# Up-projections of five of six blocks by a one-level Strassen product

## The chip, the cores and the metric

The kernel runs on one core of one Trainium2 chip. The metric is the device time of one execution in microseconds (us). Times quoted are medians. TensorE is called PE, VectorE DVE, ScalarE ACT, GpSimd POOL, and SyncE, which issues the transfers, SP.

## The reference

A Mamba-2 scan over 4 batches of 8 heads and 768 steps gives 3072 tokens of 256 features. A max-out feed-forward layer follows. Only the second part changes:

```python
def _moe_ref(x, w1, w2, w3, w_out) -> np.ndarray:      # x: 3072 x 256, w1..w3: 256 x 768, w_out: 768 x 256
    h = np.maximum(np.maximum(x @ w1, x @ w2), x @ w3)
    return (h @ w_out).astype(np.float32)
```

All of it is float32.

## The kernel before

Six blocks of 512 tokens are worked off. In each block PE runs the up-projections of its tokens (`up`), the down-projection (`down`), and between them the scan steps of the next block: transposes (`trB`, `trC`), scores (`s`), the state (`A`) and the scan's output (`y`). The order of instructions on each engine is written by hand. A bank is one tile of PSUM, the memory that PE writes its results to. A record is one entry of the trace: each float32 matmul leaves two.

```python
    def att_bank(shape, name):
        return ps.tile(shape, FP32, tag="att", bufs=5, name=name)
    def ffn_bank(shape, name):
        return ps.tile(shape, FP32, tag="ffn", bufs=3, name=name)
    # ... cut ...
    def up(c, f):                       # 128 of the 768 hidden features, 512 tokens
        # ... cut ...
        for i in range(3):              # w1, w2, w3
            p = ffn_bank([P, BLK], "up")
            for k in range(KD):         # two halves of the 256 input features
                nc.tensor.matmul(
                    out=p, lhsT=w_sb[i][:, k, f * P:(f + 1) * P], rhs=yT[c][:, k],
                    start=(k == 0), stop=(k == KD - 1))
            if i == 0:
                m = ffn.tile([P, BLK], FP32, tag="m", bufs=3, name="m")
                nc.scalar.copy(out=m, in_=p)
            else:
                nc.vector.tensor_tensor(
                    out=m if i == 1 else hT[c][:, f], in0=m, in1=p, op=ALU.max)
            fill()                      # a piece of decoding or of the scan's decays, on ACT and POOL
    def down(c, u):
        o = ffn_bank([P, 2, DM], "o")
        for i in range(2):
            # ... cut ...
            for f in range(NF):
                nc.tensor.matmul(
                    out=o[:, i], lhsT=hT[c][:, f, b * P:(b + 1) * P], rhs=wo_sb[:, f],
                    start=(f == 0), stop=(f == NF - 1), skip_group_check=True)
```

In the first block the weights are also decoded, by ACT, DVE and POOL in turn, while PE already multiplies.

## Time and profile before

| | |
|---|---|
| time, median of 3 | 320.5 us |
| span of the profiled execution | 318.6 us |
| PE busy | 303.2 us, 95% |
| DVE, ACT, POOL busy | 36%, 35%, 17% |
| one block in the middle | 48.6 us, PE never waits |

In the profile a group is a source line with its engine and tiles: "out<-in" names the tiles, "x" counts instructions; "idle before" is the time in which the engine waited just ahead of them, and the releaser is what ended it.

### The profile page before, as it was taken

Reading aid. Unit: us, or ns where it says so; the run is one execution under the profiler, and the core shown is the slowest. Engines: PE = TensorE matmul, PEld = TensorE weight load, DVE = VectorE, ACT = ScalarE, POOL = GpSimd, SP = SyncE. Lnnn points to the kernel's source line nnn. Section 1 sums busy time; section 2 is a strip of 40 time slices with the busy share of each in tenths; the row PEclk is TensorE's granted clock in tenths of the full one; section 3 lists DMA queues with packets and bytes.
Section 4 is the critical chain, followed back from the end, with each engine's and each line's share of the span. In section 5 each row is a group of like instructions: output and inputs, shape, how many; then the busy total and the mean of one; then the engine's idle time right before and its main releaser. Section 6 shows DMA issues by size and latency. Waiting matters only on the chain.

```text
span 318.6 us, 4456 instructions
## 1 busy us (share of the span) xinstructions
PE 303.2 (95%) x1746; PEld 173.7 (55%) x1746; DVE 113.2 (36%) x189; ACT 112.5 (35%) x276; POOL 54.0 (17%) x58
## 2 busy tenths in 40 slices
PE   6779998969999999999999999999999999999995
PEld 4533453458444478544468544468544468544474
DVE  2697673930133440123540123540023540023110
ACT  2857369534640264240174240084331001110100
POOL 5134563570000340000250000150000000000000
PEclk9999999979999999999999999999999999999999
DMA  8996989991798001569001569001000001000001
GB/s 90 244 389 177 173 245 197 198 106 35 196 170 97 0 1 35 161 174 128 1 0 35 147 185 129 2 2 35 33 1 0 0 2 35 33 0 0 0 0 66
DMA packets 105012, 28.06 MB, mean 88 GB/s; under 512 B 75296, under 2 KB 101920, under 8 KB 104992
## 3 DMA queue, kind: packets, MB, share of 16 engines
q1 hardware_dynamic: 104688, 27.66, 41.5%
q8 instruction: 13, 0.21, 0.3%
q10 hardware_dynamic: 304, 0.13, 0.1%
q14 instruction: 7, 0.06, 0.1%
HBM read 24.54 MB, written 3.24 MB: 87 GB/s over the span
## 4 chain that ended last, share of the span: by engine, by line
PE 82%; DVE 6%; ACT 4%; DMA 2%; POOL 2%; issue 1%; SPq 1%; ACTq 0%; DVEq 0%; POOLq 0%
PE up L502 51%; PE o L519 20%; PE y L479 3%; PE s L449 3%; DVE L L458 2%; PE y L471 2%; ACT L L367 2%; PE spread L298 1%; DMA E<-cums 1%; DVE w_u L158 1%; POOL w_u L167 1%; ACT w_u L157 1%; DVE w L170 1%; ACT CT L399 1%; PE trC L388 1%
## 5 line engine op out<-in xcount | busy, mean ns | idle before, releaser
L502 PE MATMUL up<-yT,w 128*128 128x512 f32 x432 | 190.2, 595 | 1.5 <-DVE w L170 1.5
L502 PEld LDWEIGHTS up<-yT,w 128*128 128x128 f32 x432 | 80.7, 190 | 98.4 <-issue 90.2
L519 PE MATMUL o<-wo,h 128*128 128x256 f32 x288 | 67.2, 390 | 3.2 <-DVE wo L170 3.2
L519 PEld LDWEIGHTS o<-wo,h 128*128 128x128 f32 x288 | 54.9, 194 | 14.2 <-DVE wo L170 4.0
L509 DVE TENSOR_TENSOR m<-m,up 128x512 f32<-128x512 f32 x36 | 24.7, 687 | 100.0 <-PE up L502 71.7
L507 ACT COPY m<-up 128x512 f32<-128x512 f32 x36 | 21.0, 584 | 106.4 <-PE up L502 106.4
L367 ACT ACTIVATE L<-L,ncums 128x128 f32<-128x128 f32 x160 | 48.8, 390 | 12.6 <-POOL L L363 12.6
L509 DVE TENSOR_TENSOR h<-m,up 128x512 f32<-128x512 f32 x36 | 24.7, 687 | 29.1 <-PE up L502 28.8
L458 DVE TENSOR_TENSOR L<-s,L 128x512 f32<-128x512 f32 x48 | 29.7, 682 | 3.5 <-PE s L449 3.5
L523 ACT COPY ob<-o 128x512 f32<-128x512 f32 x12 | 7.0, 585 | 49.4 <-PE o L519 41.4
L167 POOL TENSOR_TENSOR w_u<-w_u,w_r 128x512 uint32<-128x512 uint32 x12 | 18.1, 1505 | 31.3 <-DVE w_u L161 30.3
L363 POOL TENSOR_SCALAR_AFFINE_SELECT L<-L 128x1024 f32<-128x1024 f32 x20 | 21.6, 1112 | 0.0
L449 PE MATMUL s<-CT,BT 32*128 32x256 f32 x192 | 14.3, 399 | 2.9 <-ACT CT L399 2.9
L449 PEld LDWEIGHTS s<-CT,BT 32*128 32x128 f32 x192 | 9.3, 184 | 11.4 <-issue 6.8
L435 POOL TENSOR_TENSOR old<-S,E 128x256 f32<-128x256 f32 x4 | 2.5, 619 | 74.5 <-issue 74.5
L479 PE MATMUL y<-L,raw_x 128*32 128x128 f32 x384 | 13.7, 275 | 1.2 <-DVE L L458 1.1
L485 DVE COPY yT<-y 128x512 f32<-128x512 f32 x5 | 3.5, 692 | 31.7 <-PE y L479 31.7
L479 PEld LDWEIGHTS y<-L,raw_x 128*32 128x32 f32 x384 | 10.5, 109 | 4.1 <-DVE L L458 3.2
L438 POOL TENSOR_TENSOR S<-S,old 128x256 f32<-128x256 f32 x4 | 3.2, 800 | 47.7 <-DVE S L430 47.7
L158 DVE TENSOR_SCALAR w_u<-w_u 128x512 f32<-128x512 f32 x12 | 6.7, 555 | 10.9 <-ACT w_u L157 10.9
L485 ACT COPY yT<-y 128x512 f32<-128x512 f32 x7 | 4.0, 586 | 11.6 <-PE y L479 11.6
L157 ACT ACTIVATE w_u<-rb 128x512 f32<-128x512 f32 x12 | 8.0, 670 | 0.1
(66 smaller groups left out, 111.9 us busy)
## 6 DMA issues: line engine op xcount, KB each, us to landing
L<-cums SPq DMA_DIRECT2D x10, 1024.0 KB, 9.1
rb<-in_moe_w_dram SPq DMA_DIRECT2D x9, 512.0 KB, 7.7
raw_x<-in_x_dram SPq DMA_DIRECT2D x6, 512.0 KB, 7.3
out_dram<-ob SPq DMA_DIRECT2D x12, 256.0 KB, 2.1
raw_B<-in_B_dram SPq DMA_DIRECT2D x6, 256.0 KB, 4.3
raw_C<-in_C_dram SPq DMA_DIRECT2D x6, 256.0 KB, 6.2
rb<-in_moe_w_out_dram SPq DMA_DIRECT2D x3, 512.0 KB, 5.7
E<-cums SPq DMA_DIRECT2D x40, 32.0 KB, 4.0
```

Of the source, the lines that this page charges most:

```text
L157: nc.scalar.activation(u.bitcast(FP32), hi.bitcast(FP32), AF.Abs)
L158: nc.vector.tensor_scalar(out=u.bitcast(FP32), in0=u.bitcast(FP32), scalar1=SMALL, scalar2=LARGE, op0=ALU.max, op1=ALU.min)
L167: nc.gpsimd.tensor_tensor(out=u, in0=u, in1=r, op=ALU.add)
L363: nc.gpsimd.affine_select(out=L[:, b], in_=L[:, b], pattern=[[0, NH], [1, P]], compare_op=ALU.is_ge, fill=MASKED, base=0, channel_multipli ...
L367: nc.scalar.activation(L[:, b, h], L[:, b, h], AF.Exp, bias=ncum[c][:, b * NH + h:b * NH + h + 1], scale=1.0)
L449: nc.tensor.matmul(out=banks[r][:, i].rearrange("j g i -> j (g i)"), lhsT=st["BT"][rows, b], rhs=st["CT"][rows, b].rearrange("p g i -> p ( ...
L458: nc.vector.tensor_tensor(out=M, in0=banks[r], in1=M, op=ALU.mult)
L479: nc.tensor.matmul(out=ys[t][q * D:(q + 1) * D, b], lhsT=st["x"][:, b * NH + h], rhs=M[:, b, h], start=(c == 0 and b == 0), stop=True, til ...
L502: nc.tensor.matmul(out=p, lhsT=w_sb[i][:, k, f * P:(f + 1) * P], rhs=yT[c][:, k], start=(k == 0), stop=(k == KD - 1))
L507: nc.scalar.copy(out=m, in_=p)
L509: nc.vector.tensor_tensor(out=m if i == 1 else hT[c][:, f], in0=m, in1=p, op=ALU.max)
L519: nc.tensor.matmul(out=o[:, i], lhsT=hT[c][:, f, b * P:(b + 1) * P], rhs=wo_sb[:, f], start=(f == 0), stop=(f == NF - 1), skip_group_check ...
```

## The change

Strassen's scheme makes a product of two 2x2 block matrices from 7 block products in place of 8, at the price of sums before and after. Here the blocks are 128x128 of weights by 128x256 of tokens. The sums of weights (`wsum`) are made once, those of tokens (`T`) once a block, and the results are combined by DVE. Three of the four banks of a unit are accumulated on further: product 6 goes onto product 1, product 4 onto product 7, product 3 onto product 5. What ACT copies of products 1 and 6 together is called s2, and DVE's sum of s2 and product 7 is u3. Between the accumulation steps the partial sums are read, so products depend on each other through ACT and DVE; the scan steps are placed between them. Five units of one or two such groups of seven products make up a block.

```diff
-    wraw = ctx.enter_context(tc.tile_pool(name="wraw", bufs=9))
+    wraw = ctx.enter_context(tc.tile_pool(name="wraw", bufs=7))
-        return ps.tile(shape, FP32, tag="att", bufs=5, name=name)
+        return ps.tile(shape, FP32, tag="att", bufs=4, name=name)
+    def own_bank(tag, shape, name):
+        return ps.tile(shape, FP32, tag=tag, bufs=2 if tag == "u" else 1, name=name)
-            r = wtmp.tile(shape, U32, tag="w_r", name="w_r")
+            r = wtmp.tile(shape, U32, tag="w_r", bufs=1, name="w_r")
# ... cut: weight sums, T, and the bookkeeping of a unit ...
+        def p6(self):
+            self.product(6, "u")                       # onto product 1
+            self.s2 = self.kept("s2")                  # ACT copies the bank
+            u3 = ffn.tile([P, 2, HBLK], FP32, tag="u3", bufs=1, name="u3")[:, 0:self.w]
+            nc.vector.tensor_tensor(
+                out=u3, in0=self.banks["e"][:, 0:self.w], in1=self.s2, op=ALU.add)
+            self.result(1, 1, "d", u3)
+        def p4(self):
+            self.product(4, "e")                       # onto the bank that u3 reads
+            self.result(1, 0, "e", self.s2)
# ... cut ...
+        for n, unit in enumerate(units):
+            follows = units[n + 1] if n + 1 < len(units) else None
+            unit.p6()
+            fill()
+            if follows:
+                follows.p1()
+            between[n][0]()                            # a scan step
+            unit.p4()
+            unit.p3()
+            behind = between[n][1:]
+            for step in behind[0:2]:                   # scan weights, on DVE
+                step()
+            if follows:
+                follows.p7()
+                follows.p5()
+                follows.p2()
+            maxima()                                   # the maxima over w1, w2, w3, put off to here
+            for step in behind[2:]:
+                step()
# ... cut: in block 1 ...
+            weight_sums(0, nc.vector)
             scan_weights(1, 2, scan_scores(1, 2))
```

Block 1 keeps the plain up-projection. Blocks 2 to 6 use the products.

More of the change, by code (lines that the diff above doesn't have):

```diff
@@ L56 @@
     BLK = NB * P
+    HBLK = BLK // 2
+    NQ = NF // 2
     QH = P // D
@@ L73, in att_bank @@
     def att_bank(shape, name):
-        return ps.tile(shape, FP32, tag="att", bufs=5, name=name)
+        return ps.tile(shape, FP32, tag="att", bufs=4, name=name)
+    def own_bank(tag, shape, name):
+        return ps.tile(shape, FP32, tag=tag, bufs=2 if tag == "u" else 1, name=name)
+    turns = []
     def ffn_bank(shape, name):
-        return ps.tile(shape, FP32, tag="ffn", bufs=3, name=name)
+        turns.append(None)
+        return own_bank(("u", "d", "u", "e")[(len(turns) - 1) % 4], shape, name)
     a_rows = a.rearrange("b h s -> (b h) s")
@@ L376 @@
     yT = {}
+    sides = {}
     def scan_b(c, bank):
@@ L453, in scan_scores, with scan_weight, scan_old @@
         return banks
+    def scan_weight(c, b0, r, bank):
+        M = Ls[c][:, b0:b0 + 2, 2 * r:2 * r + 2]
+        nc.vector.tensor_tensor(out=M, in0=bank, in1=M, op=ALU.mult)
     def scan_weights(c, b0, banks):
         for r in range(NP):
-            M = Ls[c][:, b0:b0 + 2, 2 * r:2 * r + 2]
-            nc.vector.tensor_tensor(out=M, in0=banks[r], in1=M, op=ALU.mult)
-    def scan_out(c):
+            scan_weight(c, b0, r, banks[r])
+    def scan_old(c, bs):
         st = blocks[c]
-        M = Ls[c]
-        yT[c] = ffn.tile([P, KD, BLK], FP32, tag="yT", name="yT")
-        ys = [att_bank([P, NB, P], "y") for _ in range(KD)]
+        if "y" not in st:
+            st["y"] = [att_bank([P, NB, P], "y") for _ in range(KD)]
         if c > 0:
+            ys = st["y"]
             Sp = states[c]
-            for b in range(NB):
+            for b in bs:
                 for r in range(NP):
@@ L475, in scan_out @@
                         skip_group_check=True)
+    def scan_out(c):
+        st = blocks[c]
+        M = Ls[c]
+        ys = st["y"]
+        yT[c] = ffn.tile([P, KD, BLK], FP32, tag="yT", bufs=1, name="yT")
         for b in range(NB):
@@ L485, in scan_out @@
             copy(out=yT[c][:, t], in_=ys[t].rearrange("p b i -> p (b i)"))
+        if c > 0:
+            y11, y12, y21, y22 = (
+                yT[c][:, k, r * HBLK:(r + 1) * HBLK] for k in range(2) for r in range(2))
+            late = [ys[k].rearrange("p b i -> p (b i)")[:, r * HBLK:(r + 1) * HBLK]
+                    for k in range(2) for r in range(2)]
+            t = ffn.tile([P, 4, HBLK], FP32, tag="T", bufs=1, name="T")
+            for k, (a1, a0) in enumerate((
+                    (late[1], y11), (late[3], t[:, 0]), (late[3], y12), (late[2], t[:, 1]))):
+                nc.vector.tensor_tensor(out=t[:, k], in0=a1, in1=a0, op=ALU.subtract)
+            sides[c] = {1: y11, 2: y21, 3: y22, 4: t[:, 3], 5: t[:, 0], 6: t[:, 1], 7: t[:, 2]}
     hT = {}
@@ L496, in up @@
         if f == 0:
-            hT[c] = ffn.tile([P, NF, BLK], FP32, tag="h", name="h")
+            hT[c] = ffn.tile([P, NF, BLK], FP32, tag="h", bufs=1, name="h")
         m = None
@@ L505, in up @@
             if i == 0:
-                m = ffn.tile([P, BLK], FP32, tag="m", bufs=3, name="m")
+                m = ffn.tile([P, BLK], FP32, tag="t", bufs=6, name="m")
                 nc.scalar.copy(out=m, in_=p)
@@ L511, in up, with weight_sums @@
             fill()
+    UNITS = [[(0, 0), (0, 1)], [(1, 0), (1, 1)], [(2, 0), (2, 1)], [(0, 2), (1, 2)], [(2, 2)]]
+    wsum = const.tile([P, 4, 3, NQ, P], FP32, name="wsum")
+    def weight_sums(i, eng):
+        a11, a12, a21, a22 = (
+            w_sb[i][:, k].rearrange("p (q g f) -> p g q f", g=2, f=P)[:, g]
+            for g in range(2) for k in range(2))
+        s1, s2, s3, s4 = (wsum[:, k, i] for k in range(4))
+        eng.tensor_tensor(out=s1, in0=a21, in1=a22, op=ALU.add)
+        eng.tensor_tensor(out=s3, in0=a11, in1=a21, op=ALU.subtract)
+        eng.tensor_tensor(out=s2, in0=s1, in1=a11, op=ALU.subtract)
+        eng.tensor_tensor(out=s4, in0=a12, in1=s2, op=ALU.subtract)
@@ new lines, in left, with __init__, product, kept @@
+    def left(k, i, q):
+        if k in (1, 2, 4):
+            g, row = {1: (0, 0), 2: (0, 1), 4: (1, 1)}[k]
+            f = 2 * q + g
+            return w_sb[i][:, row, f * P:(f + 1) * P]
+        return wsum[:, {5: 0, 6: 1, 7: 2, 3: 3}[k], i, q]
+    class Unit:
+        def __init__(self, c, n):
+            self.c, self.n = c, n
+            self.quads = UNITS[n]
+            self.w = len(self.quads)
+            self.banks = {}
+        def product(self, k, into, tag=None):
+            if tag is not None:
+                shape = [P, 2, HBLK]
+                self.banks[into] = (
+                    att_bank(shape, "p_" + into) if tag == "att" else own_bank(tag, shape, "p_" + into))
+            for j, (i, q) in enumerate(self.quads):
+                nc.tensor.matmul(
+                    out=self.banks[into][:, j], lhsT=left(k, i, q), rhs=sides[self.c][k],
+                    start=(tag is not None and j == 0), stop=True, skip_group_check=True)
+        def kept(self, name):
+            t = ffn.tile([P, 2, HBLK], FP32, tag="kept", bufs=3, name=name)[:, 0:self.w]
+            nc.scalar.copy(out=t, in_=self.banks["u"][:, 0:self.w])
+            return t
+        def result(self, g, r, into, other):
+            h = hT[self.c].rearrange("p (q g) (r t) -> p q g r t", g=2, r=2)
+            i, q = self.quads[0]
+            bank = self.banks[into][:, 0:self.w]
+            if i == 0 and q == 0:
+                nc.vector.tensor_tensor(out=h[:, 0:2, g, r], in0=bank, in1=other, op=ALU.add)
+                return
+            t = ffn.tile([P, 2, HBLK], FP32, tag="t", bufs=6, name="t")[:, 0:self.w]
+            nc.vector.tensor_tensor(out=t, in0=bank, in1=other, op=ALU.add)
+            if q == 0:
+                dst, a0, a1 = h[:, 0:2, g, r], h[:, 0:2, g, r], t
+            elif self.w == 2:
+                dst, a0, a1 = h[:, q, g, r], t[:, 0], t[:, 1]
+            else:
+                dst, a0, a1 = h[:, q, g, r], h[:, q, g, r], t[:, 0]
+            later.append(lambda: nc.vector.tensor_tensor(out=dst, in0=a0, in1=a1, op=ALU.max))
+        def p1(self):
+            self.product(1, "u", "u")
+            self.s1 = self.kept("s1")
+        def p2(self):
+            self.product(2, "b", "att")
+            self.result(0, 0, "b", self.s1)
+        def p5(self):
+            self.product(5, "d", "d")
+        def p7(self):
+            self.product(7, "e", "e")
+        def p6(self):
[8 more added lines that the diff above has]
+            self.result(1, 0, "e", self.s2)
+        def p3(self):
+            self.product(3, "d")
+            self.result(0, 1, "d", self.s2)
@@ new lines, with maxima, up_all @@
+    later = []
+    def maxima():
+        while later:
+            later.pop(0)()
+    def up_all(c, between):
+        hT[c] = ffn.tile([P, NF, BLK], FP32, tag="h", bufs=1, name="h")
+        units = [Unit(c, n) for n in range(len(UNITS))]
+        for p in (Unit.p1, Unit.p2, Unit.p7, Unit.p5):
+            p(units[0])
+        for n, unit in enumerate(units):
[17 more added lines that the diff above has]
+                step()
@@ L521, in down @@
                     start=(f == 0), stop=(f == NF - 1), skip_group_check=True)
-        ob = ffn.tile([P, 2, DM], FP32, tag="ob", bufs=3, name="ob")
+        ob = ffn.tile([P, 2, DM], FP32, tag="ob", bufs=2, name="ob")
         nc.scalar.copy(out=ob, in_=o)
@@ L534 @@
     spread_j((0, 1))
-    spread_banks(2, (att_bank, ffn_bank))
+    spread_banks(2, 2 * [ffn_bank])
     spread_i((2,), True)
@@ L551 @@
     s01 = scan_scores(0, 0)
-    s23 = scan_scores(0, 2, [att_bank] + 3 * [ffn_bank])
+    s23 = scan_scores(0, 2, 4 * [ffn_bank])
     scan_weights(0, 0, s01)
@@ L556 @@
     decode()
+    scan_old(0, ())
     scan_out(0)
-    for _ in range(6):
+    for _ in range(4):
         fetch()
@@ L565 @@
     decay_load(1)
+    fetch()
+    fetch()
     load(1, "B")
@@ L590 @@
                 d[2], lambda: (sign(), d[3](), d[4]()), decode, d[5], decode, d[6], decode, d[7]]
-    for c in range(NC):
-        n = c + 1
-        for k, (g, i) in enumerate(pieces):
-            if g is down:
-                sign()
-            g(c, i)
-            if c == 0 and k == 1:
-                first_tokens()
-                scan_state(0)
-            if n < NC:
-                in_, s01, s23, state, out_ = (3, 4, 5, 5, 6) if c == 0 else (1, 3, 5, 4, 6)
-                if k == in_:
-                    scan_b(n, att_bank)
-                    scan_c(n, att_bank)
-                    if n < NC - 1:
-                        scan_bd(n)
-                if k == max(in_, s01 - 2 * (c > 0)):
-                    scan_cd(n)
-                if k == s01:
-                    scan_weights(n, 0, scan_scores(n, 0))
-                if k == s23:
-                    scan_weights(n, 2, scan_scores(n, 2))
-                if k == state and n < NC - 1:
-                    scan_state(n)
-                if k == out_:
-                    scan_out(n)
-            if n + 1 < NC and k == 4:
-                decay_load(n + 1)
-                last_load(n + 1)
-                load(n + 1, "B")
-                load(n + 1, "C")
-                load(n + 1, "x")
-                fillers += decays_of(n + 1)
@@ new lines, in loads @@
+    def loads(c):
+        if c < NC:
+            load(c, "B")
+            load(c, "C")
+            last_load(c)
+            decay_load(c)
+            load(c, "x")
+            fillers.extend(decays_of(c))
+    for k, (g, i) in enumerate(pieces):
+        if g is down:
+            sign()
+        g(0, i)
+        if k == 1:
+            first_tokens()
+            scan_state(0)
+        if k == 3:
+            scan_b(1, att_bank)
+            scan_c(1, att_bank)
+            scan_bd(1)
+        if k == 4:
+            scan_cd(1)
+            scan_weights(1, 0, scan_scores(1, 0))
+            loads(2)
+        if k == 5:
+            weight_sums(0, nc.vector)
+            scan_weights(1, 2, scan_scores(1, 2))
+            scan_state(1)
+        if k == 6:
+            scan_old(1, range(NB))
+            scan_out(1)
+            weight_sums(1, nc.gpsimd)
+            weight_sums(2, nc.vector)
@@ new lines, in transposed, with scores, weighted @@
+    def transposed(c):
+        if c < NC:
+            scan_b(c, att_bank)
+            scan_c(c, att_bank)
+            scan_cd(c)
+            if c < NC - 1:
+                scan_bd(c)
+    transposed(2)
+    for c in range(1, NC):
+        n = c + 1
+        held = {}
+        def scores(k):
+            held[k] = scan_scores(n, k)
+        loads(n + 1)
+        def weighted(k):
+            return [lambda r=r: scan_weight(n, k, r, held[k][r]) for r in range(NP)]
+        steps = [(nothing,)] * len(UNITS)
+        if n < NC:
+            steps = [
+                (lambda: scores(0), *weighted(0)),
+                (lambda: scan_state(n) if n < NC - 1 else None,),
+                (lambda: transposed(n + 1),),
+                (lambda: scores(2), *weighted(2)),
+                (lambda: scan_old(n, (0, 1)), lambda: scan_old(n, (2, 3))),
+            ]
+        up_all(c, steps)
+        down(c, 0)
+        if n < NC:
+            scan_out(n)
+        down(c, 1)
```

## The prediction

> **What bounds the kernel now.** I read the page's busy shares first, then the groups of instructions, then the chain of work in order of time, and last the timeline around one block, for latencies.
>
> ```profile
> PE 303.2 (95%) x1746; PEld 173.7 (55%) x1746; DVE 113.2 (36%) x189; ACT 112.5 (35%) x276; POOL 54.0 (17%) x58
> ...
> L502 PE MATMUL up<-yT,w 128*128 128x512 f32 x432 | 190.2, 595 | 1.5 <-DVE w L170 1.5
> ...
> L519 PE MATMUL o<-wo,h 128*128 128x256 f32 x288 | 67.2, 390 | 3.2 <-DVE wo L170 3.2
> L519 PEld LDWEIGHTS o<-wo,h 128*128 128x128 f32 x288 | 54.9, 194 | 14.2 <-DVE wo L170 4.0
> L509 DVE TENSOR_TENSOR m<-m,up 128x512 f32<-128x512 f32 x36 | 24.7, 687 | 100.0 <-PE up L502 71.7
> L507 ACT COPY m<-up 128x512 f32<-128x512 f32 x36 | 21.0, 584 | 106.4 <-PE up L502 106.4
> ```
>
> PE is the bound, DVE and ACT idle two thirds of the time. A block has 6x3x2 = 36 up matmuls and the six blocks 216, so 432 records say that each float32 matmul is two records. Means overlap (pipelining), so I take pace from the chain, here block 4 of 6:
>
> ```profile
> 177.09 10.30 PE up L502 x24
> 187.39 0.44 PE trB L388 x4
> 187.83 0.44 PE trC L388 x4
> 188.27 10.30 PE up L502 x24
> 198.57 1.08 PE s L449 x16
> 199.65 5.35 PE up L502 x12
> 204.99 0.58 PE A L423 x32
> 205.58 5.35 PE up L502 x12
> 210.92 1.08 PE s L449 x16
> 212.00 5.38 PE o L519 x24
> 217.38 1.03 PE y L471 x32
> 218.41 1.89 PE y L479 x64
> 220.29 5.38 PE o L519 x24
> ```
>
> Nothing but PE, without a gap: 48.6 us a block. A 512-column record costs 10.30/24 = 0.429 us, a 256-column record 5.38/24 = 0.224, not half of 0.429. Only the first block (to 79.9 us) has PE waits.
>
> For the waits to come I need the other engines' latencies (timeline of block 3, and a group of the forms view):
>
> ```profile
> 151.15 2.48 DVE L458 TENSOR_TENSOR L<-s,L 128x512 f32<-128x512 f32 x4 [0.44 <-PE s L449]
> 156.34 0.65 PE L423 MATMUL A<-raw_x,Bd 128*32 128x64 f32 x32
> 156.45 0.69 DVE L509 TENSOR_TENSOR h<-m,up 128x512 f32<-128x512 f32 x1 [0.96 <-PE up L502]
> 159.43 5.95 ACT L367 ACTIVATE L<-L,ncums 128x128 f32<-128x128 f32 x20
> ```
>
> ```profile
> L170 DVE SCALAR_TENSOR_TENSOR wo<-rb,w_u 128x512 uint32<-128x512 uint32 x3 | 2.0, 682 | 0.0
> ```
>
> So: DVE starts 0.11 us after the next PE work starts (156.45-156.34). One 512-wide two-input DVE operation lasts 0.69, a queue of them paces at (2.48-0.69)/3 = 0.60. A two-input operation with everything in SBUF lasts as long (0.68). An ACT copy of a bank lasts 0.58; ACT exponentials pace at 0.30. PE restarts about 0.06 after what it waited for (scores at 51.85 after the CT copies end at 51.79). For 256 columns the rows give 0.42 (state update, 128x256); its pace, by the 0.60 at 512[...], I estimate at 0.33.
>
> **What the Trainium skill says.** "VectorE: DVE Perf Modes", section "The perf-mode tier table", has tensor_tensor on float32 at 1x wherever its operands lie; the 0.60 pace from PSUM and 0.68 duration in SBUF agree, so moving the maxima to SBUF makes them no faster. "TensorE: Matmul & The Clock Gate", section "Architectural detail: the array is 16x 32x32, not 1x 128x128", calls ACT and DVE strict FIFO. The trace before cannot prove it, but everything below rests on it: a DVE instruction that is ready still waits for those queued ahead. The same page, section "LDWEIGHTS (loading the stationary operand)", gives columns/1.2 ns, 107 ns for 128; this trace shows 190 to 194 for float32, so the measurement decides. A load that long behind a 0.21 us matmul is my reading of why a 256-column record takes 0.224 and not 0.215.
>
> **The change part by part.**
>
> *Products removed.* Per block 36 matmuls of 512 columns (72 x 0.429 = 30.9 us) become 9 groups x 7 products of 256 columns, 126 records x 0.224 = 28.2 us. Gain 2.7 us a block, 13.4 us over five. The shorter moving side takes a third of the 1/8 that Strassen promises. Scan work on PE keeps its amount and only moves.
>
> *Combination added.* Before, a block needed 12 DVE maxima and 6 ACT copies. Now each of five units has four result adds, one u3 add and four maxima (five fewer in the first): 41 DVE operations, about 23 us a block, plus four subtractions. Total DVE time still fits into 50 us, so the question is where the operations stand.
>
> *The dependent products.* Product 4 accumulates onto the bank that u3 reads, so PE waits for product 6 -> ACT copy s2 -> DVE u3. Counted from the end of product 6: 0.11+0.58+0.06+0.69+0.06 = 1.50 us. In between PE has the next unit's product 1 (4 records, 0.90) and a scan step (scores 1.08, state 0.58, transposes 0.88). That would nearly cover it, and is the intent. But the DVE order of the changed kernel shows, between one unit's last result and the next unit's u3: the result of the next unit's product 2, then the four deferred maxima. That result cannot start before product 2 ends, and product 2 is just ahead of product 6. So all maxima run at the worst moment while DVE idled before. From the end of product 2:
> - DVE: 0.11 + 0.60 (result) + 4x0.60 (maxima) + 0.69 (u3) + 0.06 = 3.86.
> - PE: product 6 0.90 + product 1 0.90 + transposes 0.88 = 2.68. Wait 1.18 us (third unit).
> - Second unit: one maximum, but two scan-weight multiplies: 3.26 against 2.38, wait 0.88.
> - Fourth unit: three wide and one half maximum 3.59, against 0.90+0.45+1.08 = 2.43, wait 1.16.
> - Fifth unit, half width: 0.11+0.33+4x0.33+2x0.60 (weights)+0.42+0.06 = 3.44, against product 6 0.45 and half the old-state matmuls 0.52: wait 2.47. Its short products 5 and 2 also come too early for the banks being read: 0.40 + 0.15.
> - First unit: 1.50 against 0.90+1.08: none.
>
> *A second wait.* In the third unit the DVE multiply Cd is queued before the result of product 4. Cd waits for ACT, which first does s2, four exponentials, s1, BT, two CT and E: about 4.7 us after product 6. The result then ends at about 6.0 and frees the bank for the next product 7, which PE would reach at 4.75: 1.3 us, in blocks 2 to 4.
>
> *Sums.* Blocks 3, 4: 0.88+1.18+1.16+0.55+2.47+1.3 = 7.5 of waits less 2.7, so +4.8; adding up the stages gives +4.5, as PE work shifts a little. I take 4.5. Block 2 also holds the transposes moved forward, +5.4. Block 5 lacks state and transposes to fill with, and the Cd wait: +4.1. Block 6 has no scan step at all: waits 0.6+0.6+2.06+2.24+0.40+1.79 = 7.7, less 2.7, so +5.0. Five blocks: 5.4+4.5+4.5+4.1+5.0 = +23.5.
>
> *First block.* Eight weight sums of 384 columns go to DVE (estimate from the same pace, 0.46 each, 3.7 us; half of them ahead of the scan weights and the last decoding step that its down-projection waits for) and four to POOL; two weight loads come after the first scan loads; a single w_r buffer makes ACT wait for POOL (1.5 us per addition). Other engines already hold PE there: I put +3, with little precision.
>
> 320.5 + 23.5 + 3 = 347; I name 346.
>
> **The rivals.**
> - *PE bound throughout, as intended:* the waits are hidden and only products count: 320.5 - 13.4 + a few for the first block = 309. For it: DVE is 36% busy, and the scan steps (0.58 to 1.08) are just what covers 1.50. Against: the order of the maxima, and nothing to cover in block 6.
> - *Half hidden:* maxima run faster than 0.60, at 0.33 say. Then the second to fourth units wait some 0.1 to 0.4, the fifth about 2; near 4 a block, against 2.7 gained: about 325. Against: the 0.68 of an all-SBUF operation.
> - *DVE and POOL contend, or the clock drops:* the decode's one-input operation took 1.50 us once, where its mean is 0.555, beside a POOL addition. If POOL's masks slow the maxima so, or the granted clock, 1.00 in all later blocks, suffers from gaps of 1 to 2.5 us: 355 or more.
> - *First block decides:* the memory now taken for sums delays the decode by 5 us or more. It adds to any of the others.
>
> **Range and chances.** The gain of 13 us is nearly certain; the waits, 37 us by my sums, could be off by a third, and the first block by 3. So 332 to 357. Within 2% (314 to 327) needs the waits halved; faster by over 2% needs nearly all of them hidden. Chances: faster 0.05, within 2% 0.08, slower 0.87.
>
> **What would show it.** Product records at 0.224; in a middle block a unit-to-unit period of about 3.9+4.5 = 8.3 us; PE's idle time before product 4 ended by DVE, the largest before the fifth unit, and u3's start right at the end of a maximum or weight multiply; idle before product 7 ended by the result behind Cd; block length about 53 us, the last block's up part 36 against 30.9. I am wrong if DVE idles before u3 (then ACT or the banks set it), if PE shows no idle in blocks 3 to 6, or if the products pace below 0.21.

## The result

| | before | changed |
|---|---|---|
| time, median | 319.99 us (4 runs) | 376.54 us (4 runs, 374.79 to 379.90) |
| span, profiled execution | 318.6 us | 373.1 us |
| mean granted clock of TensorE | 0.995 | 0.929 |

The ratio is 1.178 (95% interval 1.168 to 1.189): the mean time of one kernel's fast runs over that of the other's of the same rounds, so not quite the ratio of the medians. Executions over 1.5% slower than the fastest of the same kernel are left out of the means. The change costs 56.5 us, where 25.5 were predicted and 357 was the upper end of the range.

These lines of the changed kernel's page answer to those of before: busy shares; the row of the granted clock, one digit for each fortieth of the span; and the group of product 4.

```profile
PE 313.8 (84%) x2016; PEld 232.5 (62%) x2016; DVE 203.7 (55%) x362; ACT 120.9 (32%) x296; POOL 60.5 (16%) x62
...
PEclk9989985889998989998989999989999989998899
...
L581 PE MATMUL p_e<-T,w 128*128 128x256 f32 x90 | 27.7, 427 | 36.5 <-DVE u L628 36.5
```

PE is busy 10.6 us longer than before, though it multiplies less, and idle 59 us where it was idle 15. A single releaser holds 36.5 us of that: the DVE addition u3 ahead of product 4 (`p_e<-T,w`). And the clock row has 8s in every block.

The third unit of block 3 shows both. First PE in the timeline (start, duration, engine, line, operation, tiles, size, count; in brackets the idle time before it and what ended it):

```profile
168.62 0.60 PE L397 MATMUL trB<-ident,raw_B 128*128 128x128 f32 x4
169.05 0.60 PE L397 MATMUL trC<-ident,raw_C 128*128 128x128 f32 x4
172.70 1.33 PE L581 MATMUL p_e<-T,w 128*128 128x256 f32 x4 [3.04 <-DVE u L628]
173.82 1.91 PE L581 MATMUL p_d<-yT,wsum 128*128 128x256 f32 x4
175.52 1.72 PE L581 MATMUL p_e<-T,wsum 128*128 128x256 f32 x4
```

Then DVE in the same stretch:

```profile
167.16 0.69 DVE L601 TENSOR_TENSOR t<-p_b,s 128x512 f32<-128x512 f32 x1 [2.16 <-PE p_b L581]
167.77 4.27 DVE L608 TENSOR_TENSOR h<-h,t 128x512 f32<-128x512 f32 x4
171.96 0.68 DVE L628 TENSOR_TENSOR u<-p_e,s 128x512 f32<-128x512 f32 x1
```

DVE sits idle for 2.16 us until product 2 (`p_b`) is done. Then it does that result, the four maxima, and only then u3, for which s2 had been copied by ACT at about 168.5. This is the queue order that the prediction named. New are two sizes: the maxima take 4.27 us instead of the 2.4 assumed, and after the wait of 3.04 us four product records take 1.91 us where others take 1.03.

The windows view sets the clock beside this: a middle block of the kernel before, and of the changed kernel block 1, block 3, and the 4.5 us behind that wait (the columns are busy time of each engine, then PEclk, DMA share, GB/s).

```profile
128.51:177.09 48.58, 48.58 (x290) 27.78 (x289) 14.94 (x23) 16.79 (x45) 6.58 (x7) 1.00 0.41 82
```

```profile
25.00:90.29 65.29, 55.41 (x329) 32.39 (x328) 35.45 (x65) 31.90 (x80) 29.48 (x24) 0.86 0.72 150
147.95:206.00 58.05, 50.41 (x343) 39.56 (x343) 32.77 (x56) 19.43 (x53) 7.40 (x7) 0.94 0.36 68
172.70:177.24 4.54, 4.54 (x13) 3.72 (x14) 2.65 (x4) 0.00 (x0) 0.41 (x1) 0.62 0.00 0
```

So PE was granted 0.62 of its clock right after it had idled, and 1.00 in the undisturbed block of before. A block takes 58.05 us, not the 53 predicted.

Where the 54.5 us of span went: up to the first product of block 2 PE needs 89.4 us (90.29 less 0.88 for transposes moved ahead) where it needed 79.9, +9.5. Blocks 2 to 6 with the end take 283.7 us (373.1-89.4) where they took 238.7 (318.6-79.9), +45.0.

### The profile page after: what moved, and what is told of

The parts are those of the page before. It is cut to its first block, busy times and chain, and to the rows that moved or that the text cites. A ratio compares the mean times of both kernels' runs of the same rounds, so it can differ in the third digit from the quotient of the medians.

```text
span 373.1 us, 5193 instructions
## 1 busy us (share of the span) xinstructions
PE 313.8 (84%) x2016; PEld 232.5 (62%) x2016; DVE 203.7 (55%) x362; ACT 120.9 (32%) x296; POOL 60.5 (16%) x62
## 4 chain that ended last, share of the span: by engine, by line
PE 65%; DVE 25%; ACT 3%; DMA 2%; POOL 2%; issue 2%; DVEq 0%; ACTq 0%; POOLq 0%
PE o L679 18%; PE p_e L581 13%; PE p_d L581 12%; DVE h L608 10%; PE p_b L581 5%; DVE t L601 4%; PE up L532 4%; DVE L L466 4%; PE p_u L581 3%; DVE u L628 3%; PE y L498 3%; DMA raw_B<-in_B_dram 2%; PE s L458 2%; PE y L484 1%; PE spread L306 1%
## 5 line engine op out<-in xcount | busy, mean ns | idle before, releaser
L588 ACT COPY s<-p_u 128x512 f32<-128x512 f32 (+1 forms) x50 | 26.7, 538 | 140.0 <-PE p_u L581 140.0
L679 PEld LDWEIGHTS o<-wo,h 128*128 128x128 f32 x288 | 57.3, 202 | 10.6 <-issue 1.7
L581 PE MATMUL p_e<-T,w 128*128 128x256 f32 x90 | 27.7, 427 | 36.5 <-DVE u L628 36.5
L608 DVE TENSOR_TENSOR h<-h,t 128x512 f32<-128x512 f32 (+1 forms) x60 | 37.7, 677 | 0.2
L532 PE MATMUL up<-yT,w 128*128 128x512 f32 x72 | 35.3, 649 | 2.8 <-ACT yT L504 2.8
L581 PE MATMUL p_d<-yT,wsum 128*128 128x256 f32 x90 | 29.9, 460 | 0.0
L581 PE MATMUL p_e<-T,wsum 128*128 128x256 f32 x90 | 28.0, 434 | 0.0
L532 PEld LDWEIGHTS up<-yT,w 128*128 128x128 f32 x72 | 14.6, 208 | 21.4 <-issue 17.4
L581 PE MATMUL p_d<-T,wsum 128*128 128x256 f32 x90 | 24.3, 388 | 0.7 <-DVE t L601 0.7
L581 PE MATMUL p_b<-yT,w 128*128 128x256 f32 x90 | 23.9, 384 | 0.0
L581 PE MATMUL p_u<-T,wsum 128*128 128x256 f32 x90 | 23.5, 379 | 0.0
L581 PE MATMUL p_u<-yT,w 128*128 128x256 f32 x90 | 23.5, 379 | 0.0
```

The costliest lines, as they stand in the source:

```text
L532: nc.tensor.matmul(out=p, lhsT=w_sb[i][:, k, f * P:(f + 1) * P], rhs=yT[c][:, k], start=(k == 0), stop=(k == KD - 1))
L581: nc.tensor.matmul(out=self.banks[into][:, j], lhsT=left(k, i, q), rhs=sides[self.c][k], start=(tag is not None and j == 0), stop=True, sk ...
L588: nc.scalar.copy(out=t, in_=self.banks["u"][:, 0:self.w])
L608: later.append(lambda: nc.vector.tensor_tensor(out=dst, in0=a0, in1=a1, op=ALU.max))
L679: nc.tensor.matmul(out=o[:, i], lhsT=hT[c][:, f, b * P:(b + 1) * P], rhs=wo_sb[:, f], start=(f == 0), stop=(f == NF - 1), skip_group_check ...
```

## The experiments

Eleven kernels ran. All but one compute the right result.

**Maxima ahead of the next unit's product 2.**

```diff
             if follows:
                 follows.p7()
                 follows.p5()
+                maxima()
                 follows.p2()
-            maxima()
+            else:
+                maxima()
```

> Only the place of the deferred maxima changes: they are queued on DVE before the next unit's product-2 result, not behind it. Theory A (the order on the DVE queue makes the waits before product 4): the maxima fall into the time in which DVE idles now, u3 waits for ACT only; waits of product 4 drop from about 7 us to under 2 us a block, the half-clock stretches behind them go, 335 to 345 us, clock above 0.96. Rival B (the dependent chain product 6, ACT copy, u3 itself, or the turn of the banks, is the bound): waits stay, 368 us or more.

Measured: 349.31 us, ratio 1.093 (1.088 to 1.097), clock 0.959; the idle time before product 4 fell from 36.5 to 13.1 us. Two lines of its view of waits (total, times, longest):

```profile
PE p_e L581 <- DVE u L628: 13.1, 17, 1.8
PE p_e L581 <- DVE t L601: 2.7, 3, 1.3
```

Moving one call, with the same instructions, gives back 27 us. That is theory A, and rules out rival B: the dependent chain and the banks are the same. It came 4 us short of the range. Its trace shows why: with the longer wait gone, the DVE multiply Cd, which stands ahead of a result and waits for ACT, now holds product 7 (the second line), the "second wait" of the prediction, and four maxima in the second unit take 4.43 us.

**No masks on POOL.** Wrong result on purpose.

```diff
-        if g == 0:
+        if g == 0 and c < 2:
             nc.gpsimd.affine_select(
```

> Wrong result on purpose: POOL's triangular masks of blocks 3 to 6 are left out (POOL then reads no SBUF while DVE does the maxima). If the maxima of the third unit take 0.93 us instead of 0.60 because POOL's masks contend with them: the four maxima of that unit go from 3.8 to 4.2 us to about 2.4, the wait there from 2.6 to about 1.2, the half-clock stretch behind it goes: 362 to 371 us. If the 0.93 is the maxima's own: unchanged, 376 us.

Measured: 368.23 us, 8.3 less than the changed kernel's 376.54. The same four maxima of the third unit, and the wait that they cause:

```profile
164.37 2.49 DVE L608 TENSOR_TENSOR h<-h,t 128x512 f32<-128x512 f32 x4
```

```profile
167.51 1.13 PE L581 MATMUL p_e<-T,w 128*128 128x256 f32 x4 [1.26 <-DVE u L628]
```

The maxima are back at 0.60 each, the wait is 1.26 us (the prediction had 1.18), and the four records behind it take 1.13, not 1.33. So POOL's masks had slowed the maxima. The Trainium skill, "SBUF — State Buffer", section "Who interferes with whom", states that a DVE instruction with two SBUF inputs contends with a GpSimd instruction that reads SBUF; this trace agrees, 4.27 against 2.49 us. The prediction knew of it as a rival and left it out of its sum.

**More work for PE.** Product 1 of three units a block is computed twice, into the same bank, before it is read.

```diff
             self.product(1, "u", "u")
+            if self.n > 1:
+                self.product(1, "u", again=True)       # start flag set again: the same values
             self.s1 = self.kept("s1")
```

> Product 1 of the third to fifth unit is computed twice into the same bank (2.15 us of extra PE work a block, 10.8 us in all, same result), so PE idles less in front of product 4. Theory C (gaps drop the granted clock, and the half-clock products that follow cost 1.5 to 3 us a block): no slower, 362 to 376 us, clock up from 0.93. Rival D (the lower clock costs nothing because PE would wait anyway; or the clock falls for another reason): unchanged clock, 376 to 387 us.

Measured: 366.21 us, ratio 1.143 (1.140 to 1.146), clock 0.958; one of the four runs, 370.49, counts as slow. PE does 10.8 us more and the kernel is 10.3 us faster. The same place in block 3:

```profile
168.84 1.13 PE L581 MATMUL p_e<-T,w 128*128 128x256 f32 x4 [0.40 <-DVE u L630]
169.81 1.03 PE L581 MATMUL p_d<-yT,wsum 128*128 128x256 f32 x4
```

The wait is 0.40 us and the next four records take 1.03, not 1.91. The useless products only fill time in which PE would have idled, and keep the clock. That is theory C, and rules out rival D. Part of the gain may also come from DVE getting time, since the repeat pushes everything behind it back; the 0.88 us saved on these four records alone is the clock's. The page of this run says the same of the whole: PE is busy 315.5 us, only 1.7 more than in the changed kernel, though 10.8 us of records were added, so the other records took some 9 us less. The Trainium skill, "TensorE: Matmul & The Clock Gate", section "Why this matters for your kernels", advises no PE idle gaps over about 3 us. In the changed kernel the gap of 2.2 us before the fifth unit of block 3 was already followed by slow records; its gaps of 1.1 us were not.

**The first block alone.** Pools, banks, sums and block 1 of the changed kernel, but plain up-projections in blocks 2 to 6.

```diff
-        up_all(c, steps)
-        down(c, 0)
-        ...
+        for k, (g, i) in enumerate(pieces):            # the loop of the kernel before
+            g(c, i)
+            ...
```

> Pools, first block, weight sums and T as in the changed kernel, but blocks 2 to 6 with the plain up-projection and the old order of scan steps. If the first block's own loss is what its trace shows: 328 to 331 us, the first up of block 2 at about 89 us and later blocks near 48.6 us as before. Rival: the first block only looked slow and catches up, or the 4 scan banks hurt every block: 320 us, or 340 and more.

Measured: 330.54 us, ratio 1.033 (1.028 to 1.037). The later blocks are at 48.6 us again (90.24 to 138.82 from one first up-projection to the next) and the loss of some 10 us is all in block 1. Two of its waits stand out, in the view of waits (total, times, longest):

```profile
PE s L458 <- DVE Cd L417: 4.8, 1, 4.8
PE A L432 <- DVE L L466: 3.6, 1, 3.6
```

**Each of the two waits taken away.** For the first, the scores take their fourth bank elsewhere and Cd comes later:

```diff
-            scan_cd(1)
-            scan_weights(1, 0, scan_scores(1, 0))
+            scan_weights(1, 0, scan_scores(1, 0, 3 * [att_bank] + [ffn_bank]))
+            scan_cd(1)
```

> As the run with the plain up-projection, but in block 1 the fourth scores bank is taken from the up-projection's banks and Cd is done behind the scan weights, so that scores no longer wait for Cd to read the bank of trC. If that wait (4.8 us, and the half-clock products behind it, some 2 us) is the larger part of the first block's loss: 323 to 327 us against 330.5. If other work in the block fills the gap anyway: 329 or more.

Measured: 325.37 us. For the second, the sums of w1 go behind the scan weights:

```diff
-            weight_sums(0, nc.vector)
             scan_weights(1, 2, scan_scores(1, 2))
         if k == 6:
+            weight_sums(0, nc.vector)
             scan_old(1, range(NB))
```

> As the run with the plain up-projection, but the four DVE weight sums of w1 are queued behind the scan weights and the first down-projection of block 1 instead of ahead of them. If they cause the wait of the state product A (3.5 us, and the half-clock down products behind it, 2.2 us): 325 to 328 us against 330.5. If A waits for something else: unchanged.

Measured: 325.59 us. Each gives about 5 us of the 10, as expected, and neither is hidden by the rest of the block; the two were not taken away together in this kernel. With 4 banks for the scan in place of 5 the scores waited until Cd had read the bank of trC (the edit moves the bank and Cd, so it does not part the two); the four sums, 3.1 us on DVE with POOL reading beside them, stood in front of what frees the bank of A.

**All causes taken away at once.** Both of the first-block edits; and in a unit, product 2 of the next unit also runs ahead of product 4, scan steps follow product 3, the maxima follow the last result, the masks are loaded later, and two thirds of a down-projection are drawn ahead of the fifth unit's product 4.

```diff
             unit.p6()
-            fill()
             if follows:
                 follows.p1()
-            between[n][0]()
+            pre[n]()                                    # fifth unit: down-projection, four of six steps
+            if n == 4:
+                maxima()                                # of the fourth unit
+            if follows:
+                follows.p2()
+            fill()
             unit.p4()
             unit.p3()
-            ...
+            post[n]()                                   # scan step
+            if n != 3:
+                maxima()
             if follows:
                 follows.p7()
                 follows.p5()
-                follows.p2()
-            maxima()
```

> The Strassen kernel with the causes taken away: both first-block changes of the two runs beside it; products 1 and 2 of the next unit both ahead of product 4; scan steps behind product 3; maxima behind the last result of their unit; masks late in the block; the first four steps of the down-projection ahead of product 4 of the fifth unit. Theory A with C (queue order and clock were the loss, the product count is a real gain: 126 records of 0.2155 us for 72 of 0.429, 3.7 us a block): 303 to 316 us, clock above 0.98. Rival E (the DVE's 41 operations a block, or dependent products, cannot be hidden by any order): 325 us or more.

Measured: 318.34 us median. The runs spread, 314.13 to 319.51, with clocks from 0.984 down to 0.973, and two of the four count as slow. The ratio, 0.993 (0.989 to 0.997), is not that of the two fast ones alone, 314.13 and 317.23: their mean of 315.7 is 0.984 of the 321.0 of the kernel before. In the faster profiled execution one wait is left:

```profile
147.72 1.03 PE L581 MATMUL p_b<-yT,w 128*128 128x256 f32 x4
151.40 1.13 PE L581 MATMUL p_e<-T,w 128*128 128x256 f32 x4 [2.65 <-DVE u L628]
```

DVE stood at Cd, waiting for ACT's exponential, with the second unit's maxima queued behind; these took 3.81 us, again beside POOL. Behind this gap of 2.65 us the records ran at full clock; so a gap of that length sets the clock down sometimes, not always. Rival E is ruled out. The fast runs lie in the range given and 1 us above it, the median of all four is 2 us above it.

**Cd one unit later.**

```diff
-            transposed(n + 1)                           # second unit, with scan_cd in it
+            scan_b(n + 1, att_bank)
+            scan_c(n + 1, att_bank)
+            post[2] = lambda: scan_cd(n + 1)            # third unit
```

> As the best order so far, but the DVE multiply Cd is queued one unit later, so that the four maxima of the second unit no longer stand behind its wait for ACT. The last PE waits of 1.3 to 2.7 us a block in front of product 4 of the third unit (blocks 2 to 4) should go: theory A 306 to 312 us against 318.3 (profiled execution 314.1), all executions in one state, since no gap is left that lowers the clock. If the maxima are slow only because POOL reads SBUF at that time: 313 us or more.

Measured: 311.28 us, ratio 0.971 (0.968 to 0.974), all six runs 309.39 to 312.28. All PE waits before product 4 together are 1.1 us, and from 88 to 270 us of its span the granted clock was 1.00, where block 3 of the changed kernel had 0.94; what clock it still loses lies in the first block (0.91 from 25 to 88 us). This is faster than both kernels, with the same 126 product records a block as the changed kernel.

**A control of a number in the prediction.** The kernel before, its down-projection alternating between the two output halves:

```diff
-        for i in range(2):
-            ...
-            for f in range(NF):
+        fill(); fill()
+        for f in range(NF):
+            for i in range(2):
-                    start=(f == 0), stop=(f == NF - 1), skip_group_check=True)
+                    start=(f == 0 and i == 0), stop=(f == NF - 1), skip_group_check=True)
```

> The kernel before with one change: the down-projection alternates between its two output halves from record to record instead of accumulating twelve records into one half in a row. It tests why a 256-column record took 0.224 us there but 0.2155 as a Strassen product, where consecutive pairs go to different halves. If back-to-back accumulation into the same columns is what costs: down records at 0.2155, 12 x 24 x 0.0085 = 2.4 us less, 318 us. If the weight load (as the prediction had it) or the changing moving side costs: 0.224, 320.5 us.

Measured: 316.77 us, ratio 0.988 (0.987 to 0.990), but not for the reason given. In the chain of work the 24 records still take 5.38 us:

```profile
65.16 1.99 PE o L520 x8
...
207.51 5.38 PE o L520 x24
```

So the test of the pace failed: accumulating in a row costs nothing. Looking closer at the trace of before settles it otherwise. In the down-projection from 211.93 us the 21st record starts at 216.35 and the 24th at 217.00 (from views cut off at these times), 0.217 each; the first four are spaced by 0.24. The 5.38 us hold 24 x 0.2155 = 5.17 and some 0.2 us of change-over to and from other work. The gain came from block 1: there the kernel before had 16 records left to do after it had waited for the last decoded weights, at 66.23 us, and this one has 8 (first line), since the first eight records of the second half no longer stand behind the wait. That is 1.7 us of the 4.5 by which block 2 starts earlier (75.44 against 79.94). Some 1.7 more is the clock: behind its wait of 2.8 us the kernel before needs 5.41 us for its 16 records, at a clock of 0.68, where 16 x 0.2155 is 3.45; the 8 take 1.99, 0.3 above pace. And the wait ends 1.1 us earlier (65.16), for a reason not looked into.

**The same in the best kernel**, with the state product between the two parts:

```diff
+        if k == 6:
+            down_part(0, 0, range(4))
+            scan_state(1)
+            down_part(0, 0, range(4, NF))
+            down_end(0, 0)
+        else:
+            g(0, i)
```

> As the run with Cd moved, plus in block 1 the finding of the alternated down-projection: the first four steps of both output halves run ahead of the step that waits for the last decoded weights, and the state product stands between them instead of ahead. If the 2.6 us wait of the state product and the half-clock down products behind it go: 3 to 5 us less than 311.3, that is 306 to 309 us. If the first block is held by the decoding on ACT, DVE and POOL whatever PE does: 310 or more.

Measured: 309.17 us, ratio 0.963 (0.959 to 0.967), six runs, clock 0.986 to 0.994. It is the best kernel, 3.7% faster than the kernel before. Part of that is the alternated down-projection, which helps the plain kernel too: against its 316.77 us the products are worth 7.6 us, 2.4%. It gained 2.1 us over the run with Cd moved, less than the 3 to 5 expected. (One execution of the kernel before in these rounds took 977.5 us, and nothing here explains it.) A block, in its chain of work, from one first product to the next:

```profile
127.42 0.86 PE p_u L581 x4
128.28 0.86 PE p_b L581 x4
...
173.16 0.86 PE p_u L581 x4
```

That is 45.7 us where before had 48.6.

**A second w_r buffer.**

```diff
-            r = wtmp.tile(shape, U32, tag="w_r", bufs=1, name="w_r")
+            r = wtmp.tile(shape, U32, tag="w_r", bufs=2, name="w_r")
-            t = ffn.tile([P, 2, HBLK], FP32, tag="t", bufs=6, name="t")[:, 0:self.w]
+            t = ffn.tile([P, 2, HBLK], FP32, tag="t", bufs=5, name="t")[:, 0:self.w]
```

> As the run beside it, plus a second w_r buffer (paid for with one buffer less for the combined results). If the single w_r buffer that the change left costs the decoding ACT's waits for POOL (2.2 to 2.8 us at the first up): 1 to 3 us less than the run beside it. If the five result buffers now hold DVE, or decoding is not on the path: same or slower.

Measured: 309.04 us. No difference, so the single buffer that the change left costs nothing that this can show.

## Why the prediction was wrong, point by point

*Direction and order held.* The kernel is slower, and the largest single part of the loss has the reason named: deferred maxima stand between product 2 and u3 on DVE's queue. One moved call gave back 27 us.

*The waits before product 4* were sized well. The prediction's list sums to 31.5 us over five blocks: 5.7 in each of blocks 2 to 4, 7.3 in block 6, and 7.2 in block 5 (the same terms with the state and the transposes missing). The profile has 36.5. In block 3 the four waits were predicted as 0.88, 1.18, 1.16, 2.47 and measured as 1.07, 3.04, 1.15, 2.22. The second is the one that was off, because "DVE and POOL contend" was put among the rivals; without masks it is 1.26. With all other waits counted, the prediction had 37 us and the changed kernel idles 37.2 in blocks 2 to 6. That so close a match came out is partly luck: the Cd waits (3 x 1.3) did not come, and the waits behind slow maxima were longer instead.

*The price of PE's own work was the step that failed.* The sum multiplied every record by its full-clock pace, added the waits at their length, and kept "the granted clock, 1.00 in all later blocks" as something that only a rival would touch. For a change of work it had only the little that 0.224 holds above the bare pace. In fact the waits that the prediction itself forecast lower it. Adding up, in the chain of block 3, what pieces took beyond the same pieces at full clock: 0.20+0.85+0.46 behind the 3.04 us wait, 0.54+0.64 behind the 2.22 us wait, 2.7 us. Likewise about 2.7 in blocks 2 and 4, 1.2 in block 5, 2.5 in block 6, and 4.5 in block 1, where the 12 up-projection records behind the scores take 7.2 us instead of 5.35: an estimate of 16 us in all, 11.8 of it in blocks 2 to 6. (The kernel before loses some 2 us in the same way in its first block, so about 14 are the change's.) The run with doubled products shows the effect itself, the sum only its rough size.

*The first block* was put at +3 and cost 9.5 us. The prediction named the sums ahead of the scan weights. It missed the fifth scan bank. Bank and place of Cd are 5 us, the sums 5 us (both with the slow records behind them), and the single w_r buffer, tested in the best kernel, nothing, as three runs show.

*The product pace* of 0.224 us was too high: 0.2155. The gain is 30.9-27.15 = 3.75 us a block, not 2.7. The weight load was the wrong reason for 0.224: the product records have one each too, of 190 ns, and keep to 0.2155. The excess was change-over time, spread over the records.

*The second wait*, at Cd, is missing in the changed kernel and present, at up to 1.3 us, in the run with the maxima moved (and in block 3, at 0.83 and 0.95 us, in those without masks and with doubled products): in the changed kernel u3 came so late that ACT was done in time. Two waits on one path do not add.

*What remains.* Block 3 took 9.5 us more. Products give -3.75, waits +7.7 (with 0.2 at product 5), the clock +2.7; about 2.8 us are left. They lie in many change-overs: four records behind a change of work or a wait take 1.05 to 1.13 us rather than 0.86. In part these are short waits for a bank: in three units of block 3 product 7 starts 0.06 us after DVE's last read of the bank that it takes (at 164.20, the read from 163.45 lasting 0.69). Over blocks 2 to 6 the loss of 45.0 us is -18.7 for the products, +37.2 for waits, some +11.8 for the clock, and about 14.7 are left. The prediction had 23.5 us there. Its waits came out, and its 0.224 held 5.4 us of the change-overs, so of the 21.5 us that it missed some 11.8 are the clock and some 9.3 the change-overs. The clock as a cause is shown by the run with doubled products; the change-overs were taken apart by no run, and their cause stays open.

*The rival "as intended"* gave 309 us for waits all hidden. The order that hides them measures 309.2, though with a better pace and a better first block than that sum assumed, so the match is luck. (A slip in the prediction: the first unit has four maxima fewer, not five; its 41 operations are right.)

## What to carry to other kernels

When fewer products are bought with dependent sums, write down, for each wait of the busy engine, the whole queue of the engine it waits for, and move everything that is not needed there out of the way: here 67 us, between 376.5 and 309.2, lay in the order of instructions and the turn of banks, with the same products. Price a gap on TensorE at more than its length, because the records behind it can run at a lower clock. And take the cost of an instruction from the middle of a run of its kind, not from the length of the whole piece.

## What the Trainium skill lacked or had wrong

- "TensorE: Matmul & The Clock Gate", section "Why this matters for your kernels": the advice is to avoid idle gaps above about 3 us. A gap of 2.2 us was followed by slow records here and one of 2.65 us in another kernel was not; with the maxima moved, two gaps of 0.8 and 0.9 us close together were followed by a down-projection of 6.2 us instead of 5.4. The page's section on PSUM-queue cycling does say that frequent short idles make the clock swing, but no section gives their length or cost; the changed kernel lost an estimated 16 us to slow records.
- The same page, section "LDWEIGHTS (loading the stationary operand)": 107 ns by its formula, 190 to 194 ns for float32 in the trace before. They did not set the pace: 256-column products ran at 0.2155 us a record.
- "SBUF — State Buffer", section "Who interferes with whom", is right on DVE and GpSimd. It quotes slowdowns of 6.8 times for DVE and 1.5 times for GpSimd, but does not say for which instructions. Here four maxima went from 2.49 to 4.27 us, 1.7 times, beside POOL's masks.
